# One DMA per v pair, quartered first weights, split zero fills, later loads of the second expert and a halved last tile in a sparse-attention and mixture kernel

## The chip, the cores and the metric

The kernel runs on one core of a Trainium2 chip. The metric is the device time of one execution, in microseconds (us). Before the change it was 744.33 us, the median of 3 runs (744.23 to 744.38).

The engines are called as the profile calls them: PE (TensorE matmul), PEld (its weight load), DVE (VectorE), ACT (ScalarE), POOL (GpSimd), SP (SyncE). Every run here was fast: none was over 1.5% above the fastest of its kernel. Within the fast runs there is still one difference that matters for a change of 0.3%: each run lists its mean granted TensorE clock, and some show 0.988 to 0.998 instead of 0.999 to 1.000. I call runs at 0.999 and above "full-clock" runs and always say when I use only those.

## The reference, cut to what matters

```python
# attention: 4 batches, 8 heads, 768 positions, 64 columns
k_sum = k.reshape(B, H, nb, 32, D).max(axis=3)       # block maxima of k
v_sum = v.reshape(B, H, nb, 32, D).mean(axis=3)      # block means of v
# scores: a window of |i - j| < 16, and the 24 blocks; one softmax over both
out = softmax([local scores, block scores + log(32)]) @ [v, v_sum]
# experts: x = out as 3072 x 512, E = 8, F = 1024
P = sinkhorn(exp(x @ w_gate), 8 rounds)
for e in range(8):
    out += P[:, e:e+1] * (relu(x @ w1[e]) @ w2[e])
```

## The kernel before

The heads are taken in 16 pairs. All work of the attention, of expert 0 and of the normalisation of P is put in order at build time by a small planner: each unit has an engine, an estimated cost and dependencies, and each engine then runs its own list in that fixed order. Experts 1 to 7 follow as a plain loop.

The parts that change:

```python
        def load_v(i):                                   # two DMAs per pair, one per head
            b, h0 = i // PB, (i % PB) * 2
            for j in range(2):
                nc.gpsimd.dma_start(out=v_x[i % NQ][:, :, j, 0:D],
                                    in_=v[b, h0 + j].rearrange("(g p) d -> p g d", p=128))
        # ...
        def keep_busy(n):                                # an idle (filler) matmul
            t = bank("m", "idle")
            for _ in range(n):
                nc.tensor.matmul(t[:], lhsT=zeros[:, 0:128], rhs=zeros[:], start=True, stop=True)
        nc.vector.memset(zeros, 0.0)
        keep_busy(14)                                    # 14 at the start
        # ...
        def late_constants():                            # one block on DVE
            for t in E_e:
                nc.vector.memset(t[64:128, :, :], 0.0)
            for t in V_e:
                nc.vector.memset(t[:], 0.0)
                nc.vector.memset(t[0:24, :, D:VD], 32.0)
                nc.vector.memset(t[32:56, :, VD + D:2 * VD], 32.0)
            nc.vector.memset(col_en, float(E) / float(N))
        # ...
        load(("w1", 0), lambda: load_w1(0, 0, 2), 0.85, 2.5)     # expert 0's w1 in halves
        for i in range(PB):
            load_pair(i, "r")                                    # second half of q
        load(("w1", 1), lambda: load_w1(0, 1, 2), 0.85, 2.5)
        # ...
        def transposed():                # POOL touches pair 12's k and q, then loads expert 1
            r = (NP - 4) % NB
            nc.gpsimd.tensor_copy(out=warm[:, 0:1], in_=kT[r][0:1, 0:1])
            nc.gpsimd.tensor_copy(out=warm[:, 1:2], in_=qT[r][0:1, W:W + 1])
        # ...
        plan.idle = (0.43, lambda: keep_busy(2), U["rl", 0, 0])  # planner: two fillers where
                                                                 # it foresees a gap over 0.43
        # ...
            yp = mps.tile([128, 512], FP32, tag="m", name="yps")     # experts 1 to 7, one tile
            project_mm(e, yp, h, c, range(KF))
            nc.vector.scalar_tensor_tensor(out=out_acc[:, t, :], in0=yp[:],
                                           scalar=P_sb[:, t, e:e + 1], in1=out_acc[:, t, :],
                                           op0=ALU.mult, op1=ALU.add)
            if e == E - 1:
                nc.sync.dma_start(out=out[t * 128:(t + 1) * 128, :], in_=out_acc[:, t, :])
```

The softmax here doesn't subtract the row's maximum and nothing guards it: scores larger than these inputs give would overflow.

Of the kernel before, what the change touches and what calls it, by code (L numbers as in the profile page):

```python
# [9 lines left out]
FP32 = mybir.dt.float32  # L10
BF16 = mybir.dt.bfloat16
AF = mybir.ActivationFunctionType
ALU = mybir.AluOpType
# [99 lines left out]
def kernel(  # L113
# [10 lines left out]
    nc = tc.nc  # L124

    B, H, S, D = q.shape
    G = S // 128
# [31 lines left out]
    col_en = const.tile([128, 128], FP32)  # L159
    warm = const.tile([1, 8], FP32)  # L160
    zeros = const.tile([128, 512], BF16)
# [46 lines left out]

    def project_mm(e, yp, h, c, fs):
        for f in fs:  # L210
            nc.tensor.matmul(yp[:], lhsT=h[:, f, c * 128:(c + 1) * 128],  # L211
                             rhs=w2s[e][:, f, :], start=(f == 0), stop=(f == KF - 1))

# [6 lines left out]
    with tc.tile_pool(name="attn", bufs=1) as attn, \  # L220
# [7 lines left out]
        ksT = [attn.tile([128, 128], BF16, name=f"ksT{i}") for i in range(NB)]  # L228
        v_x = [attn.tile([128, G, 2, VD], BF16, name=f"vx{i}") for i in range(NQ)]

# [36 lines left out]
        def load_v(i):  # L267
            b, h0 = i // PB, (i % PB) * 2
            for j in range(2):
                nc.gpsimd.dma_start(out=v_x[i % NQ][:, :, j, 0:D],  # L270
                                    in_=v[b, h0 + j].rearrange("(g p) d -> p g d", p=128))

# [55 lines left out]
        def block_sums(i):  # L328
            sv = v_x[i % NQ]
            vs = at["vs", i] = bank("a", "vs")[:, 0:2 * D]  # L330
            for g in range(G):
                nc.tensor.matmul(vs.rearrange("p (j d) -> p j d", j=2), lhsT=m_blk[:, g, :],  # L332
                                 rhs=sv[:, g, :, 0:D], start=(g == 0), stop=(g == G - 1))

# [11 lines left out]
        def near_values(i):  # L346

            sv, ve = v_x[i % NQ], V_e[i % NE]
            eng = nc.sync if i < BY_DMA else nc.gpsimd
            for j in range(2):  # L350
                c0, q0 = VD * j, 64 + 32 * j
                eng.dma_start(out=ve[q0 + W:q0 + 2 * W, 1:G, c0:c0 + VD],
                              in_=sv[128 - W:128, 0:G - 1, j, :])
                eng.dma_start(out=ve[q0:q0 + W, 0:G - 1, c0:c0 + VD],
                              in_=sv[0:W, 1:G, j, :])

# [47 lines left out]
        def values(i, h):  # L404
            sv, ee, ve, em = v_x[i % NQ], E_e[i % NE], V_e[i % NE], at["em", i]
            av = at["av", i, h] = bank("a", "av")
            for cc in range(HG):
                c, o = HG * h + cc, cc * 2 * VD
                for j in range(2):
                    nc.tensor.matmul(av[:, o + j * VD:o + (j + 1) * VD],  # L410
                                     lhsT=em[:, j, c, :], rhs=sv[:, c, j, :],
                                     start=(cc == 0 and j == 0), stop=False,
                                     skip_group_check=True)
            for cc in range(HG):
                c, o = HG * h + cc, cc * 2 * VD
                nc.tensor.matmul(av[:, o:o + 2 * VD], lhsT=ee[:, c, :], rhs=ve[:, c, :],  # L416
                                 start=False, stop=True, skip_group_check=True)
# [46 lines left out]
        def values_h(i, h):  # L464
            sv, em, es = v_x[i % NQ], E_h[(PB * h + i) % NEH], at.pop(("es", i, h))
            av = at["av", i, h] = bank("a", "av")

            def mm(p0, p1, cc, j, lhsT, rhs, n=VD, start=False, stop=False):
                o = cc * 2 * VD + j * VD
                nc.tensor.matmul(av[p0:p1, o:o + n], lhsT=lhsT, rhs=rhs, start=start, stop=stop,  # L470
                                 skip_group_check=True)

            for cc in range(HG):
                for j in range(2):
                    mm(0, 128, cc, j, em[:, j, cc, 2 * W:2 * W + 128], sv[:, HG * h + cc, j, :],
                       start=(cc == 0 and j == 0))
            for cc in range(HG):
                c = HG * h + cc
                for j in range(2):
                    if c + 1 < G:  # L480
                        mm(96, 128, cc, j, em[0:32, j, cc + 1, 0:32], sv[0:32, c + 1, j, :])
                    if c > 0:
                        mm(0, 32, cc, j, em[96:128, j, cc - 1 if cc else HG, LIVE:PADL],
                           sv[96:128, c - 1, j, :])
            for cc in range(HG):
                mm(0, 128, cc, 0, es[:, cc, :], V_s[i][:], n=2 * VD, stop=True)
# [129 lines left out]

        def late_constants():
            for t in E_e:
                nc.vector.memset(t[64:128, :, :], 0.0)
            for t in V_e:  # L620
                nc.vector.memset(t[:], 0.0)
                nc.vector.memset(t[0:24, :, D:VD], 32.0)
                nc.vector.memset(t[32:56, :, VD + D:2 * VD], 32.0)
            nc.vector.memset(col_en, float(E) / float(N))

# [9 lines left out]
        def load_pair(i, parts="kqv"):  # L635
            old = i - NQ
            for c in parts:
                if c == "v":
                    load(("v", i), lambda: load_v(i), 1.65, 1.75,
                         [U.get(("A", old, 1)), U.get(("near", old))])  # L640
                elif i < PB and c in "qr":
                    h = "qr".index(c)
                    load(("q", i, h), lambda h=h: load_qk(i, 1, h), 0.65, 0.6)
                else:
                    z = "kq".index(c)
                    load((c, i), lambda z=z: load_qk(i, z), 0.75 if i < PB else 1.65,
                         1.1 if i < PB else 1.55, [U.get(("tr", old, z)), U.get(("tr", old, 2))])

        def pair_start(i, prio):
# [9 lines left out]
            for z in range(0 if i >= BY_DMA else 1 if i < PB else 2):  # L659
# [9 lines left out]
            U["vs", i] = add("PE", 0.4, lambda: block_sums(i),  # L669
                             [U["v", i]] + ([U.get(("A", i - NE, 1))] if i >= PB else []), prio + 0.01, opens=[buf])  # L670
            U["Vs", i] = add("DVE", 0.22 if i < PB else 0.7, lambda: block_out(i), [U["vs", i]],
# [35 lines left out]
        def pair_whole(i, prio):  # L707
            U["near", i] = add("SP" if i < BY_DMA else "POOL", 2.4 if i < BY_DMA else 3.0, lambda: near_values(i),
                               [U["v", i], U.get(("A", i - NE, 1))], prio, lag=3.5)
            x1 = []  # L710
# [14 lines left out]
            for h in range(2):  # L725
                U["mk", i, h] = add("DVE", 0.56, lambda h=h: masks(i, h),
                                    [U["X", i, h], *x1[:h], U.get(("A", i - 2, 1))], prio)
            U["ed", i] = add("DVE", 0.78, lambda: edges(i),
                             [U["X", i, 0], U["X", i, 1], U["mk", i, 1], U.get(("A", i - NE, 1))], prio)
            for h in range(2):  # L730
# [22 lines left out]
        def expert0(t0, xs):  # L753
            key, n = t0, len(halves)
            halves.append(key)
            pr = 1000.0 + n
            w = [U["w1", 0], U["w1", 1]]
            evac, old = [], [U.get(("pj", halves[n - 2], c)) for c in range(HG)] if n >= 2 else []
            for f in range(KF):
                buf = Buffer("m")  # L760

                def fn(f=f):
                    at["hp", key, f] = hidden0(key, t0, f)
                m = add("PE", 0.67, fn, xs + [w[f // 4]] + old, pr + f * 0.01, opens=[buf])

# [30 lines left out]
        load_pair(3, "v")  # L796
        load(("w1", 0), lambda: load_w1(0, 0, 2), 0.85, 2.5)
        for i in range(PB):
            load_pair(i, "r")
        load(("w1", 1), lambda: load_w1(0, 1, 2), 0.85, 2.5)  # L800
        load("w2", lambda: load_w2(0), 0.85, 5.0)
        add("DVE", 4.0, constants, [], -5.0)
        for i in range(PB):
            pair_start(i, i)
            pair_half(i, 0, i)
        add("DVE", 1.8, late_constants, [U["A", PB - 1, 0]], 5.5)
        expert0(0, [U["x", i, 0] for i in range(PB)])
# [14 lines left out]
        def transposed():  # L822

            r = (NP - 4) % NB
            nc.gpsimd.tensor_copy(out=warm[:, 0:1], in_=kT[r][0:1, 0:1])
            nc.gpsimd.tensor_copy(out=warm[:, 1:2], in_=qT[r][0:1, W:W + 1])

        last[0] = add("POOL", 0.3, transposed, [last[0]] + [U["kT", NP - 4, z] for z in range(2)])
        load("w1n", lambda: load_w1(1), 0.85, 5.0)
# [28 lines left out]
    def step2(e, n):  # L858
        h = hs.pop((e, n))
        for c in range(4):  # L860
            t = 4 * n + c
            if e == 1:
                nc.vector.tensor_scalar_mul(out=out_acc[:, t, :], in0=out_acc[:, t, :],
                                            scalar1=P_sb[:, t, 0:1])
            yp = mps.tile([128, 512], FP32, tag="m", name="yps")
            project_mm(e, yp, h, c, range(KF))
            nc.vector.scalar_tensor_tensor(out=out_acc[:, t, :], in0=yp[:],  # L867
                                           scalar=P_sb[:, t, e:e + 1], in1=out_acc[:, t, :],
                                           op0=ALU.mult, op1=ALU.add)
            if e == E - 1:  # L870
                nc.sync.dma_start(out=out[t * 128:(t + 1) * 128, :], in_=out_acc[:, t, :])

# [35 lines left out]
```

## Time and profile before

| | before |
|---|---|
| time, median | 744.33 us |
| span of the profiled run | 742.2 us |
| first hidden matmul of expert 0 | 25.4 us |
| first hidden matmul of expert 1 | 157.7 us |
| end of the last matmul to end of span | 4.15 us |

From the profile page of before (line 1 is the span; then PE's busy time; then its busy tenths and the granted clock in 40 slices):

```profile
span 742.2 us, 10242 instructions
...
PE 729.8 (98%) x4292; PEld 358.3 (48%) x4364; DVE 373.5 (50%) x734; ACT 201.0 (27%) x343; POOL 90.6 (12%) x118
...
PE   8999999999999999999999999999999999999997
...
PEclk9999999999999999999999999999999999999999
```

PE is 90% busy or more in all slices but the first and the last. The Trainium skill says that this is not the whole story ("Trainium Kernel Development and Optimization", "Best Practices": the distance to roofline is not to be judged by matmul busy time). I use the pitch, the time from one matmul's start to the next: 32 matmuls of 512 columns take 6.91 us in the chain, 0.216 us each, which agrees with the gap that "TensorE: Matmul & The Clock Gate" (Part 1, "Wait — 56ns, not 53.3ns?") gives for a warm array (N/2.4 + 2.5 ns).

Busy time by stretches of before, in us. The columns are the length, then busy time and (instructions) of PE, PEld, DVE, ACT and POOL, the granted clock, the DMA engines' mean busy time and GB/s:

```profile
core 0: us, PE busy (x) PEld busy (x) DVE busy (x) ACT busy (x) POOL busy (x), PEclk, DMA share, GB/s
0.00:31.50 31.50, 27.35 (x398) 16.06 (x401) 22.99 (x113) 17.82 (x29) 23.57 (x37) 1.00 1.35 150
31.50:92.00 60.50, 59.86 (x721) 39.91 (x724) 55.48 (x147) 43.65 (x73) 54.57 (x69) 1.00 1.89 122
92.00:155.00 63.00, 62.34 (x536) 38.15 (x541) 45.53 (x122) 37.98 (x73) 1.56 (x2) 1.00 0.22 37
155.00:700.00 545.00, 542.37 (x2477) 247.11 (x2526) 232.74 (x332) 96.76 (x163) 10.92 (x11) 1.00 0.16 28
```

The slack is in the first line: PE is idle 4.15 us of 31.5 us there. Do not read the last line as 2.6 us of idle time in experts 1 to 7. The trace of before has 4292 matmul records beside 4364 weight loads, one of which belongs to each matmul, and a missing record looks like a short gap. The same holds for 25 recorded idle matmuls of 28 issued.

POOL's issues of loads at the start of before (start, duration, engine, line, operation, tile):

```profile
2.72 1.67 POOL L270 DMA_DIRECT2D vx_109<-in_v_dram  x2
...
4.69 0.74 POOL L258 DMA_DIRECT2D kst<-in_k_dram  x1
...
8.01 1.68 POOL L270 DMA_DIRECT2D vx_110<-in_v_dram  x2
...
10.34 0.66 POOL L258 DMA_DIRECT2D qst<-in_q_dram  x1
```

Two v issues take 1.67 us together, and k and q of the following pairs stand behind them.

The chain of waits of before (start, duration, what) has the zero fills as a block on DVE from 24.16 to 26.72 us, around the first work of expert 0 (25.41 us) and just before a masked product ("av") that waits for DVE:

```profile
24.16 0.38 DVE Ee_122 L619
...
24.56 0.38 DVE Ee_123 L619
...
25.84 0.39 DVE Ve_125 L621
...
26.72 0.41 DVE qT_97 L202
...
27.75 0.93 PE av L470 x19
```

Then the first hidden matmul of expert 0 and of expert 1, from the timeline of PE of before, and the last tile's end, with the last eviction on DVE:

```profile
25.41 0.82 PE L206 MATMUL hps<-xT,w_402 128*128 128x384 bf16 x4
```

```profile
157.74 2.54 PE L206 MATMUL hps<-xT,w_2019 128*128 128x512 bf16 x11
```

```profile
733.79 4.26 PE L211 MATMUL yps<-w_5682,h 128*128 128x512 bf16 x18
...
738.10 0.75 DVE L867 SCALAR_TENSOR_TENSOR out_acc<-yps,P_sb,out_acc 128x512 f32<-128x512 f32 x1 [0.97 <-PE yps L211]
```

A store of the output takes 2.0 us from issue to landing, the median of 24 (the list of DMA issues of before; the columns are tile, queue, count, size, us to landing):

```profile
out_dram<-out_acc SPq DMA_DIRECT2D x24, 256.0 KB, 2.0
```

### The profile page before, as it was taken

What the parts mean: (1) busy time and instruction counts of PE and PEld (TensorE: products, weight loads), DVE (VectorE), ACT (ScalarE), POOL (GpSimd) and SP (SyncE); (2) the same over time, 40 slices, a digit from 0 to 9 for tenths busy, and PEclk for the clock granted to TensorE, in tenths of its full rate; (3) what the DMA queues carried; (4) which work ended last, traced back from release to release, by engine and by line L of the source; (5) the groups of instructions that cost most, each with busy time, mean ns of one, the idle gap of its engine ahead of it and who ended that gap; (6) DMA issues with size and microseconds to landing.
All of it is one profiled execution on the core that took longest, in us unless ns stands there. A gap on an engine that the chain in (4) does not pass through costs nothing.

```text
span 742.2 us, 10242 instructions
## 1 busy us (share of the span) xinstructions
PE 729.8 (98%) x4292; PEld 358.3 (48%) x4364; DVE 373.5 (50%) x734; ACT 201.0 (27%) x343; POOL 90.6 (12%) x118
## 2 busy tenths in 40 slices
PE   8999999999999999999999999999999999999997
PEld 4666666544444444444444444444444444444443
DVE  7789976783444444444444444444444444444443
ACT  5677676442112112111111111121121121121120
POOL 8599700010000000000000000000000000000000
PEclk9999999999999999999999999999999999999999
DMA  9999970060003300213003300212003300001212
GB/s 123 169 130 129 103 119 2 1 104 10 1 1 57 57 1 0 35 29 51 1 1 57 58 1 0 49 28 38 1 1 57 57 1 0 1 1 65 92 72 113
DMA packets 86669, 33.68 MB, mean 45 GB/s; under 512 B 68704, under 2 KB 79968, under 8 KB 86624
## 3 DMA queue, kind: packets, MB, share of 16 engines
q0 software_dynamic: 78032, 26.22, 32.7%
q1 hardware_dynamic: 8064, 6.80, 3.0%
q8 instruction: 34, 0.56, 0.3%
q14 instruction: 11, 0.09, 0.0%
q10 hardware_dynamic: 528, 0.02, 0.0%
HBM read 52.45 MB, written 6.29 MB: 79 GB/s over the span
## 4 chain that ended last, share of the span: by engine, by line
PE 93%; DVE 6%; issue 1%
PE hps L206 44%; PE yps L211 43%; DVE xs L501 1%; PE idle L570 1%; PE tkq L283 1%; DVE ks_103 L315 1%; PE av L470 1%; PE sg L324 1%; PE tx L508 1%; PE ss L422 1%; DVE em L387 1%; PE vs L332 1%; PE av L410 0%; PE av L416 0%; DVE xT L202 0%
## 5 line engine op out<-in xcount | busy, mean ns | idle before, releaser
L197 ACT ACTIVATE h<-hps 128x512 bf16<-128x512 f32 (+1 forms) x220 | 125.8, 572 | 478.9 <-PE hps L206 461.9
L211 PEld LDWEIGHTS <-h 128*128 128x128 bf16 x1536 | 149.8, 98 | 175.7
L867 DVE SCALAR_TENSOR_TENSOR out_acc<-yps,P_sb,out_acc 128x512 f32<-128x512 f32 x168 | 126.2, 751 | 166.4 <-PE yps L211 158.5
L199 DVE TENSOR_SCALAR h<-hps 128x512 bf16<-128x512 f32 (+1 forms) x180 | 122.8, 682 | 169.7 <-PE hps L206 169.4
L206 PE MATMUL hps<-xT,w_402 128*128 128x384 bf16 x256 | 48.2, 326 | 0.0
L211 PE MATMUL yps<-w_514,h 128*128 128x512 bf16 x177 | 44.5, 379 | 0.7
L206 PE MATMUL hps<-xT,w_5680 128*128 128x512 bf16 x189 | 42.3, 379 | 0.2
L211 PE MATMUL yps<-w_2042,h 128*128 128x512 bf16 x189 | 42.3, 379 | 0.2
L206 PE MATMUL hps<-xT,w_3528 128*128 128x512 bf16 x189 | 42.3, 379 | 0.2
L211 PE MATMUL yps<-w_4606,h 128*128 128x512 bf16 x188 | 42.2, 379 | 0.3
L211 PE MATMUL yps<-w_4068,h 128*128 128x512 bf16 x189 | 42.3, 379 | 0.2
L206 PE MATMUL hps<-xT,w_4066 128*128 128x512 bf16 x188 | 42.2, 379 | 0.2
L206 PE MATMUL hps<-xT,w_2966 128*128 128x512 bf16 x188 | 42.2, 379 | 0.2
L211 PE MATMUL yps<-w_5144,h 128*128 128x512 bf16 x188 | 42.2, 379 | 0.2
L211 PE MATMUL yps<-w_2968,h 128*128 128x512 bf16 x187 | 42.2, 379 | 0.3
L206 PE MATMUL hps<-xT,w_5142 128*128 128x512 bf16 x189 | 42.3, 379 | 0.2
L206 PE MATMUL hps<-xT,w_4604 128*128 128x512 bf16 x187 | 42.0, 379 | 0.2
L211 PE MATMUL yps<-w_3530,h 128*128 128x512 bf16 x188 | 42.0, 379 | 0.2
L211 PE MATMUL yps<-w_5682,h 128*128 128x512 bf16 x187 | 41.8, 379 | 0.2
L206 PE MATMUL hps<-xT,w_2019 128*128 128x512 bf16 x188 | 41.9, 379 | 0.2
L206 PEld LDWEIGHTS <-w_402 128*128 128x128 bf16 x256 | 23.7, 99 | 13.1
L206 PEld LDWEIGHTS <-w_2966 128*128 128x128 bf16 x192 | 18.8, 98 | 22.6
(249 smaller groups left out, 582.8 us busy)
## 6 DMA issues: line engine op xcount, KB each, us to landing
out_dram<-out_acc SPq DMA_DIRECT2D x24, 256.0 KB, 2.0
qst<-in_q_dram POOLq DMA_DIRECT2D x32, 96.0 KB, 4.3
kst<-in_k_dram POOLq DMA_DIRECT2D x24, 96.0 KB, 4.6
w_402<-in_moe_w_dram POOLq DMA_DIRECT2D x2, 512.0 KB, 8.2
w_514<-in_moe_w_dram POOLq DMA_DIRECT2D x1, 1024.0 KB, 12.4
w_2019<-in_moe_w_dram POOLq DMA_DIRECT2D x1, 1024.0 KB, 8.2
w_2042<-in_moe_w_dram POOLq DMA_DIRECT2D x1, 1024.0 KB, 12.5
w_2966<-in_moe_w_dram POOLq DMA_DIRECT2D x1, 1024.0 KB, 8.0
```

The lines of the kernel that those rows point to most:

```text
L197: nc.scalar.activation(out=out, in_=in_, func=AF.Relu, bias=0.0, scale=1.0)
L199: nc.vector.tensor_scalar_max(out=out, in0=in_, scalar1=0.0)
L206: nc.tensor.matmul(hp[:, 0:n], lhsT=w1s[e][:, dk, f * 128:(f + 1) * 128], rhs=xT[:, dk, t0:t0 + n], start=(dk == 0), stop=(dk == KD - 1))
L211: nc.tensor.matmul(yp[:], lhsT=h[:, f, c * 128:(c + 1) * 128], rhs=w2s[e][:, f, :], start=(f == 0), stop=(f == KF - 1))
L283: nc.tensor.transpose(t[:, g * 128:(g + 1) * 128], st[:, g, :, :].rearrange("p j d -> p (j d)"), ident)
L315: nc.vector.tensor_reduce(out=ks[i % 2][:, 0, 0:24], in_=kT[r][:].rearrange("p (n w) -> p n w", w=32), axis=AX.X, op=ALU.max)
L324: nc.tensor.matmul(dst, lhsT=kT[r][p0:p0 + 64, g * 128:(g + 1) * 128], rhs=qT[r][p0:p0 + 64, g * 128 + l0:g * 128 + l1], start=True, stop= ...
L332: nc.tensor.matmul(vs.rearrange("p (j d) -> p j d", j=2), lhsT=m_blk[:, g, :], rhs=sv[:, g, :, 0:D], start=(g == 0), stop=(g == G - 1))
L387: nc.vector.tensor_tensor(out=at["em", i][:, :, c, :], in0=at["er", i][:, :, c, W:W + 128], in1=band[:, None, None, W:W + 128].to_broadcas ...
L422: nc.tensor.matmul(ss[:, 0:HS], lhsT=ksT[r][:], rhs=qT[r][:, W + h * HS:W + (h + 1) * HS], start=True, stop=True)
L470: nc.tensor.matmul(av[p0:p1, o:o + n], lhsT=lhsT, rhs=rhs, start=start, stop=stop, skip_group_check=True)
L867: nc.vector.scalar_tensor_tensor(out=out_acc[:, t, :], in0=yp[:], scalar=P_sb[:, t, e:e + 1], in1=out_acc[:, t, :], op0=ALU.mult, op1=ALU.add)
```

## The change

Its words are: one DMA for v of a pair; transposes all on PE; expert 0's w1 in quarters; expert 1's loads wait for the last near rows; last tile in column halves. In fact, all transposes are on PE before too. The words do not mention that the zero fills are split as well. (Near rows are the rows of v beside each group of 128 positions, which are copied by DMA for the local window.) The core of the diff, with cuts:

```diff
-        v_x = [attn.tile([128, G, 2, VD], BF16, name=f"vx{i}") for i in range(NQ)]
+        v_x = [attn.tile([128, 2, G, VD], BF16, name=f"vx{i}") for i in range(NQ)]
         def load_v(i):
-            for j in range(2):
-                nc.gpsimd.dma_start(out=v_x[i % NQ][:, :, j, 0:D],
-                                    in_=v[b, h0 + j].rearrange("(g p) d -> p g d", p=128))
+            nc.gpsimd.dma_start(
+                out=v_x[i % NQ][:].rearrange("p j g x -> p (j g) x")[:, :, 0:D],
+                in_=v[b, h0:h0 + 2].rearrange("j (g p) d -> p (j g) d", p=128))
  ...  (v_x is indexed accordingly in six other places)
-        def late_constants():  ... all fills in one unit
+        def edge_constants(n):   nc.vector.memset(E_e[n][64:128, :, :], 0.0)  ... col_en for n == 0
+        def value_constants(n):  t = V_e[n]; ... the three fills of t
-                    load(("v", i), lambda: load_v(i), 1.65, 1.75,
+                    load(("v", i), lambda: load_v(i), 0.95, 1.75,          # planned cost
  ...
-        load(("w1", 0), lambda: load_w1(0, 0, 2), 0.85, 2.5)
-        for i in range(PB):
-            load_pair(i, "r")
-        load(("w1", 1), lambda: load_w1(0, 1, 2), 0.85, 2.5)
+        for n in range(4):
+            load(("w1", n), lambda n=n: load_w1(0, n, 4), 0.85, 1.25)
+            if n == 1:
+                for i in range(PB):
+                    load_pair(i, "r")
  ...
-        add("DVE", 1.8, late_constants, [U["A", PB - 1, 0]], 5.5)
+        for n in range(NE):
+            U["ec", n] = add("DVE", 0.42, lambda n=n: edge_constants(n), [U["A", PB - 1, 0]], 15 + n)
+            U["vc", n] = add("DVE", 0.5, lambda n=n: value_constants(n), [U["A", PB - 1, 0]], 15.5 + n)
  ...
-            r = (NP - 4) % NB
+            r = (NP - 1) % NB          # pair 15 instead of 12, and its near rows too
+            ve = V_e[(NP - 1) % NE]
+            for j in range(2):
+                nc.gpsimd.tensor_copy(out=warm[:, 2 + j:3 + j],
+                                      in_=ve[64 + 32 * j:96 + 32 * j, G - 2, VD * j:VD * j + 1])
  ...
-            yp = ...; project_mm(e, yp, h, c, range(KF)) ...
+            parts = 2 if (e, t) == (E - 1, NT - 1) else 1
+            for d0 in range(0, DM, DM // parts):
+                d = slice(d0, d0 + DM // parts)
+                yp = ...; project_mm(e, yp, h, c, range(KF), d)
+                ...  evict d; store d, the second half on ACT's queue
```

More of the change, by code (lines that the diff above doesn't have):

```diff
@@ L159 @@
     col_en = const.tile([128, 128], FP32)
-    warm = const.tile([1, 8], FP32)
+    warm = const.tile([32, 8], FP32)
     zeros = const.tile([128, 512], BF16)
@@ L207, in hidden_mm, with project_mm @@
                              rhs=xT[:, dk, t0:t0 + n], start=(dk == 0), stop=(dk == KD - 1))
-    def project_mm(e, yp, h, c, fs):
+    def project_mm(e, yp, h, c, fs, d=slice(0, 512)):
         for f in fs:
-            nc.tensor.matmul(yp[:], lhsT=h[:, f, c * 128:(c + 1) * 128],
-                             rhs=w2s[e][:, f, :], start=(f == 0), stop=(f == KF - 1))
+            nc.tensor.matmul(yp[:, d], lhsT=h[:, f, c * 128:(c + 1) * 128],
+                             rhs=w2s[e][:, f, d], start=(f == 0), stop=(f == KF - 1))
     NQ = 6
@@ L332, in block_sums @@
                 nc.tensor.matmul(vs.rearrange("p (j d) -> p j d", j=2), lhsT=m_blk[:, g, :],
-                                 rhs=sv[:, g, :, 0:D], start=(g == 0), stop=(g == G - 1))
+                                 rhs=sv[:, :, g, 0:D], start=(g == 0), stop=(g == G - 1))
         def block_out(i):
@@ L352, in near_values @@
                 eng.dma_start(out=ve[q0 + W:q0 + 2 * W, 1:G, c0:c0 + VD],
-                              in_=sv[128 - W:128, 0:G - 1, j, :])
+                              in_=sv[128 - W:128, j, 0:G - 1, :])
                 eng.dma_start(out=ve[q0:q0 + W, 0:G - 1, c0:c0 + VD],
-                              in_=sv[0:W, 1:G, j, :])
+                              in_=sv[0:W, j, 1:G, :])
         def scores(i):
@@ L410, in values @@
                     nc.tensor.matmul(av[:, o + j * VD:o + (j + 1) * VD],
-                                     lhsT=em[:, j, c, :], rhs=sv[:, c, j, :],
+                                     lhsT=em[:, j, c, :], rhs=sv[:, j, c, :],
                                      start=(cc == 0 and j == 0), stop=False,
@@ L474, in values_h @@
                 for j in range(2):
-                    mm(0, 128, cc, j, em[:, j, cc, 2 * W:2 * W + 128], sv[:, HG * h + cc, j, :],
+                    mm(0, 128, cc, j, em[:, j, cc, 2 * W:2 * W + 128], sv[:, j, HG * h + cc, :],
                        start=(cc == 0 and j == 0))
@@ L480, in values_h @@
                     if c + 1 < G:
-                        mm(96, 128, cc, j, em[0:32, j, cc + 1, 0:32], sv[0:32, c + 1, j, :])
+                        mm(96, 128, cc, j, em[0:32, j, cc + 1, 0:32], sv[0:32, j, c + 1, :])
                     if c > 0:
                         mm(0, 32, cc, j, em[96:128, j, cc - 1 if cc else HG, LIVE:PADL],
-                           sv[96:128, c - 1, j, :])
+                           sv[96:128, j, c - 1, :])
             for cc in range(HG):
@@ L615, in constants, with edge_constants, value_constants @@
             nc.vector.tensor_copy(out=wg_bf[:], in_=wg_f32[:])
-        def late_constants():
-            for t in E_e:
-                nc.vector.memset(t[64:128, :, :], 0.0)
-            for t in V_e:
-                nc.vector.memset(t[:], 0.0)
-                nc.vector.memset(t[0:24, :, D:VD], 32.0)
-                nc.vector.memset(t[32:56, :, VD + D:2 * VD], 32.0)
-            nc.vector.memset(col_en, float(E) / float(N))
+        def edge_constants(n):
+            nc.vector.memset(E_e[n][64:128, :, :], 0.0)
+            if n == 0:
+                nc.vector.memset(col_en, float(E) / float(N))
+        def value_constants(n):
+            t = V_e[n]
+            nc.vector.memset(t[:], 0.0)
+            nc.vector.memset(t[0:24, :, D:VD], 32.0)
+            nc.vector.memset(t[32:56, :, VD + D:2 * VD], 32.0)
         U = {}
@@ L669, in pair_start @@
             U["vs", i] = add("PE", 0.4, lambda: block_sums(i),
-                             [U["v", i]] + ([U.get(("A", i - NE, 1))] if i >= PB else []), prio + 0.01, opens=[buf])
+                             [U["v", i]] + ([U.get(("A", i - NE, 1)), U["vc", i % NE]] if i >= PB else []), prio + 0.01, opens=[buf])
             U["Vs", i] = add("DVE", 0.22 if i < PB else 0.7, lambda: block_out(i), [U["vs", i]],
@@ L708, in pair_whole @@
             U["near", i] = add("SP" if i < BY_DMA else "POOL", 2.4 if i < BY_DMA else 3.0, lambda: near_values(i),
-                               [U["v", i], U.get(("A", i - NE, 1))], prio, lag=3.5)
+                               [U["v", i], U.get(("A", i - NE, 1)), U["vc", i % NE]], prio, lag=3.5)
             x1 = []
@@ L728, in pair_whole @@
             U["ed", i] = add("DVE", 0.78, lambda: edges(i),
-                             [U["X", i, 0], U["X", i, 1], U["mk", i, 1], U.get(("A", i - NE, 1))], prio)
+                             [U["X", i, 0], U["X", i, 1], U["mk", i, 1], U.get(("A", i - NE, 1)), U["ec", i % NE]], prio)
             for h in range(2):
@@ L756, in expert0 @@
             pr = 1000.0 + n
-            w = [U["w1", 0], U["w1", 1]]
+            w = [U["w1", n] for n in range(4)]
             evac, old = [], [U.get(("pj", halves[n - 2], c)) for c in range(HG)] if n >= 2 else []
@@ L763, in fn @@
                     at["hp", key, f] = hidden0(key, t0, f)
-                m = add("PE", 0.67, fn, xs + [w[f // 4]] + old, pr + f * 0.01, opens=[buf])
+                m = add("PE", 0.67, fn, xs + [w[f // 2]] + old, pr + f * 0.01, opens=[buf])
                 def ev(f=f):
@@ L822, in transposed @@
         def transposed():
-            r = (NP - 4) % NB
-            nc.gpsimd.tensor_copy(out=warm[:, 0:1], in_=kT[r][0:1, 0:1])
-            nc.gpsimd.tensor_copy(out=warm[:, 1:2], in_=qT[r][0:1, W:W + 1])
-        last[0] = add("POOL", 0.3, transposed, [last[0]] + [U["kT", NP - 4, z] for z in range(2)])
+            r = (NP - 1) % NB
+            nc.gpsimd.tensor_copy(out=warm[:, 0:1], in_=kT[r][0:32, 0:1])
+            nc.gpsimd.tensor_copy(out=warm[:, 1:2], in_=qT[r][0:32, W:W + 1])
+            ve = V_e[(NP - 1) % NE]
+            for j in range(2):
+                nc.gpsimd.tensor_copy(out=warm[:, 2 + j:3 + j],
+                                      in_=ve[64 + 32 * j:96 + 32 * j, G - 2, VD * j:VD * j + 1])
+        last[0] = add("POOL", 0.3, transposed, [last[0], U["near", NP - 1]] + [U["kT", NP - 1, z] for z in range(2)])
         load("w1n", lambda: load_w1(1), 0.85, 5.0)
@@ L864, in step2 @@
                                             scalar1=P_sb[:, t, 0:1])
-            yp = mps.tile([128, 512], FP32, tag="m", name="yps")
-            project_mm(e, yp, h, c, range(KF))
-            nc.vector.scalar_tensor_tensor(out=out_acc[:, t, :], in0=yp[:],
-                                           scalar=P_sb[:, t, e:e + 1], in1=out_acc[:, t, :],
-                                           op0=ALU.mult, op1=ALU.add)
-            if e == E - 1:
-                nc.sync.dma_start(out=out[t * 128:(t + 1) * 128, :], in_=out_acc[:, t, :])
+            parts = 2 if (e, t) == (E - 1, NT - 1) else 1
+            for d0 in range(0, DM, DM // parts):
+                d = slice(d0, d0 + DM // parts)
+                yp = mps.tile([128, 512], FP32, tag="m", name="yps")
+                project_mm(e, yp, h, c, range(KF), d)
+                nc.vector.scalar_tensor_tensor(out=out_acc[:, t, d], in0=yp[:, d],
+                                               scalar=P_sb[:, t, e:e + 1], in1=out_acc[:, t, d],
+                                               op0=ALU.mult, op1=ALU.add)
+                if e == E - 1:
+                    (nc.scalar if d0 else nc.sync).dma_start(out=out[t * 128:(t + 1) * 128, d],
+                                                             in_=out_acc[:, t, d])
     for si, (e, n) in enumerate(steps):
```

## The prediction

> **What bounds the kernel.** TensorE: the page shows PE busy 729.8 of 742.2 us at full clock. The Trainium skill ("Trainium Kernel Development and Optimization", "Best Practices") warns that matmul busy time is a bad metric, so I count columns: in the chain of waits 32 matmuls of 512 columns take 6.91 us, 0.216 us each, which is what "TensorE: Matmul & The Clock Gate" gives for a warm array (512/2.4 + 2.5 ns). Experts 1 to 7 are 2688 such matmuls, 580 us; they start at about 155 us and only the last tile changes. So the change works in the first 155 us and the last 6.
>
> Slack there, from busy time by stretches: from 0 to 31.5 us PE is busy 27.35 us (1.3 us of the gap is start-up); from 31.5 to 155 us it is idle only 1.3 us. Also 28 idle (keep-warm) matmuls run, 14 of them after the start; these cost about 3 us at 0.216. So at most about 7 us can be won.
>
> **What changes.** Despite its words, transposes do not move: all pairs are on PE already.
> 1. v in one DMA: Pool issues two per pair in 1.65 us; I estimate 1.0 for one (other issues take 0.6 to 0.9). Pool issues back to back from 34 to 86 us, but PE is filled by expert 0 then (waits list: 0.3 us for a v load), so only the first pairs matter: their k and q come 0.7 to 2 us earlier.
> 2. The zero fills of edge and value tiles, a block on DVE at 24.2 to 26.7 us on the chain, are split and interleaved. DVE work is the same; the 0.8 us weight-load wait for the mask at 27.7 should shrink.
> 3. The scheduler puts in 22 idle matmuls instead of 28: 6 x 0.216 = 1.3 us, if PE does not just wait instead.
> 4. w1 in quarters: the first half already lands at 22.4 us, before its use at 25.4; freedom, not time.
> 5. Expert 1's loads wait for pair 15's near rows (issued 107.8 to 110.4): they start at about 113 instead of 91 us and take 8 and 12.5 us, so they land by about 127, before their use at 155. No stall. Near rows of pair 13 no longer share DMA with them (5.5 us landing against 2.5 for others); PE hardly waited: at most 0.3 us.
> 6. Last tile in halves: 16 matmuls of 256 columns cost the same 1.7 us; the last eviction (0.75 us, DVE) becomes about 0.4, the last store is half as large: about 0.2 less of 2.0. About 0.5 us.
>
> **Sum on the critical path:** idle matmuls -1.3, gaps at 7 to 28 us -0.5, later gaps -0.2, tail -0.5: -2.5 us.
>
> **Prediction: 741.8 us**, 8 in 10 between 740.2 and 743.8. Faster by over 2%: 0.01; within 2%: 0.98; slower by over 2%: 0.01.
>
> **What would show it.** Right: expert 1's first hidden matmul about 2 us earlier; 22 idle matmuls and no more PE idle time before 31.5 us than now; expert loads issued near 111 us with no PE wait for them; one v issue of about 1.0 us; last eviction near 0.4 us and last PE matmul to the end of span about 3.5 instead of 4.1 us. Wrong: PE waits for v of pair 0 or 1 (block sums now come before summaries); v issue still 1.6 us; PE idle at 31 to 155 us grown, as DVE is 92% busy from 31.5 to 92 us.
>
> **What could make it wrong.** The head may be bound by DVE/ACT latency, so that removing idle matmuls only uncovers gaps: then about 743.5. Or the new order in the first half shortens more than counted: near 740. A missed weight load at 155 us would cost several us; I see none.

## The result, and the profile after

The changed kernel took 742.12 us, the median of 4 runs (741.55 to 743.85), against 744.30 for the 4 runs of before. The ratio is 0.9975 with a 95% interval of 0.9957 to 0.9992. Ratios are the mean time of one kernel's fast runs over that of the other's of the same rounds, so not quite the ratio of the medians. It is inside the 2% band, and the time is inside the predicted range (741.8; 740.2 to 743.8).

| | before | after |
|---|---|---|
| median | 744.30 | 742.12 |
| span of the profiled run | 742.2 | 739.8 |
| expert 0 begins | 25.4 | 22.3 |
| expert 1 begins | 157.7 | 155.9 |
| expert 1's begin to the end of the span | 584.5 | 583.9 |
| idle matmuls issued | 28 | 22 |

The page of the changed kernel, its first two lines (the clock row is all nines, as before):

```profile
span 739.8 us, 10282 instructions
...
PE 732.2 (99%) x4366; PEld 358.6 (48%) x4366; DVE 373.1 (50%) x735; ACT 201.3 (27%) x343; POOL 82.8 (11%) x106
```

The higher busy share here is partly an artefact: this trace has every matmul record (4366), the other does not. The span is what counts.

The same stretches of the changed kernel:

```profile
0.00:31.50 31.50, 28.69 (x419) 17.18 (x420) 24.99 (x118) 19.04 (x31) 23.75 (x37) 1.00 1.45 156
31.50:92.00 60.50, 59.62 (x719) 39.78 (x717) 54.42 (x146) 44.21 (x73) 44.55 (x52) 1.00 1.87 119
92.00:155.00 63.00, 62.69 (x532) 37.55 (x531) 45.76 (x122) 37.21 (x72) 3.58 (x7) 1.00 0.25 41
155.00:700.00 545.00, 545.00 (x2526) 247.06 (x2525) 231.64 (x330) 96.11 (x161) 10.93 (x11) 1.00 0.16 28
```

The first stretch has gained: PE is busy 28.69 us instead of 27.35, with fewer fillers in it (three fillers of before have no record, so a part of the difference is an artefact). The middle has not. Both kernels stand at about 1.2 to 1.3 us of idle time from 31.5 to 155 us, where before's figure is raised by missing records.

POOL's issues at the start of the changed kernel:

```profile
2.72 1.04 POOL L269 DMA_DIRECT2D vx_109<-in_v_dram  x1
...
4.12 0.71 POOL L258 DMA_DIRECT2D kst<-in_k_dram  x1
...
7.43 1.05 POOL L269 DMA_DIRECT2D vx_110<-in_v_dram  x1
...
9.14 0.64 POOL L258 DMA_DIRECT2D qst<-in_q_dram  x1
```

One v DMA takes 1.04 us instead of 1.67 for two, so k of pair 1 goes out 0.57 us earlier, v of pair 1 0.58 us and q of pair 3 1.2 us (the prediction had 0.7 to 2). Not everything lands earlier: the first pair's v, now one load of twice the size, lands 5.9 us after its issue, at 8.6 us, while the two halves of before had landed by 8.3 us. Pair 1's v lands at 13.6 us, and at 14.0 us or later in before. The first hidden matmuls of expert 0 and expert 1:

```profile
22.31 0.82 PE L206 MATMUL hps<-xT,w_347 128*128 128x384 bf16 x4
```

```profile
155.90 4.48 PE L206 MATMUL hps<-xT,w_2427 128*128 128x512 bf16 x20
```

Expert 0 begins 3.1 us earlier, expert 1 only 1.84 us earlier. The difference is no loss by itself, since the order around these points differs; only at expert 1's begin have both kernels done the same useful work.

The chain of waits of the changed kernel now runs through POOL's issues and the landing of pair 1's v:

```profile
6.85 0.59 POOL qst L258
7.43 6.14 DMA vx_110<-in_v_dram
...
13.62 0.50 PE vs L332 x6
```

Block sums ("vs") of pair 1 start at 13.62 us, when that DMA, issued at 7.43 us, has landed. Up to there the chain is POOL and v. The wait of PE for a mask behind the zero-fill block (0.4 us at 27.75 us in before) is no longer listed, but the chain still passes through two of the four split units on DVE, from 21.27 to 22.56 us.

The end of the changed kernel, and its DMA issues for v and for the last tile:

```profile
736.27 0.48 DVE L879 SCALAR_TENSOR_TENSOR out_acc<-yps,P_sb,out_acc 128x256 f32<-128x256 f32 x1 [0.39 <-PE yps L211]
736.79 0.36 ACTq L883 DMA_DIRECT2D out_dram<-out_acc  x1
```

```profile
vx_109<-in_v_dram POOLq DMA_DIRECT2D x3, 192.0 KB, 5.9
...
out_dram<-out_acc SPq DMA_DIRECT2D x1, 128.0 KB, 1.8
out_dram<-out_acc ACTq DMA_DIRECT2D x1, 128.0 KB, 1.8
```

The last eviction is 0.48 us instead of 0.75, the last store lands in 1.8 us instead of 2.0, and the span ends about 3.55 us after the last matmul's end instead of 4.15.

Expert 1's loads are now issued at 116 us, from POOL's timeline of the changed kernel:

```profile
115.97 0.76 POOL L187 DMA_DIRECT2D w_2427<-in_moe_w_dram  x1
116.72 0.90 POOL L193 DMA_DIRECT2D w_2449<-in_moe_w_dram  x1
```

They take 8.0 and 13.6 us to land, and the first use is at 155.9 us, so PE does not wait for them.

### The profile page after: what moved, and what is told of

The parts are those of the page before. It is cut to its first block, busy times and chain, and to the rows that moved or that the text cites. A ratio compares the mean times of both kernels' runs of the same rounds, so it can differ in the third digit from the quotient of the medians.

```text
span 739.8 us, 10282 instructions
## 1 busy us (share of the span) xinstructions
PE 732.2 (99%) x4366; PEld 358.6 (48%) x4366; DVE 373.1 (50%) x735; ACT 201.3 (27%) x343; POOL 82.8 (11%) x106
## 4 chain that ended last, share of the span: by engine, by line
PE 93%; DVE 4%; DMA 1%; POOL 1%; issue 0%; POOLq 0%
PE hps L206 44%; PE yps L211 44%; DMA vx_110<-in_v_dram 1%; DVE xs L501 1%; PE tkq L283 1%; PE sg L324 1%; PE ss L422 1%; PE av L470 1%; PE tx L508 1%; PE vs L332 1%; DVE em L387 1%; DVE ks_103 L315 0%; DVE ks_104 L315 0%; PE av L416 0%; PE av L410 0%
## 5 line engine op out<-in xcount | busy, mean ns | idle before, releaser
L879 DVE SCALAR_TENSOR_TENSOR out_acc<-yps,P_sb,out_acc 128x512 f32<-128x512 f32 (+1 forms) x169 | 126.4, 748 | 165.9 <-PE yps L211 165.8
L211 PE MATMUL yps<-w_501,h 128*128 128x512 bf16 x192 | 46.2, 379 | 0.0
L211 PE MATMUL yps<-w_2947,h 128*128 128x512 bf16 x192 | 42.4, 379 | 0.0
L211 PE MATMUL yps<-w_4047,h 128*128 128x512 bf16 x192 | 42.4, 379 | 0.0
L211 PE MATMUL yps<-w_2449,h 128*128 128x512 bf16 x192 | 42.4, 379 | 0.0
L211 PE MATMUL yps<-w_4585,h 128*128 128x512 bf16 x192 | 42.4, 379 | 0.0
L211 PE MATMUL yps<-w_5123,h 128*128 128x512 bf16 x192 | 42.4, 379 | 0.0
L211 PE MATMUL yps<-w_3509,h 128*128 128x512 bf16 x192 | 42.4, 379 | 0.0
L211 PE MATMUL yps<-w_5661,h 128*128 128x512 bf16 (+1 forms) x200 | 42.3, 370 | 0.0
## 6 DMA issues: line engine op xcount, KB each, us to landing
w_2449<-in_moe_w_dram POOLq DMA_DIRECT2D x1, 1024.0 KB, 13.6
```

Of the source, the lines that this page charges most:

```text
L211: nc.tensor.matmul(yp[:, d], lhsT=h[:, f, c * 128:(c + 1) * 128], rhs=w2s[e][:, f, d], start=(f == 0), stop=(f == KF - 1))
L879: nc.vector.scalar_tensor_tensor(out=out_acc[:, t, d], in0=yp[:, d], scalar=P_sb[:, t, e:e + 1], in1=out_acc[:, t, d], op0=ALU.mult, op1=A ...
```

## The experiments

All kernels gave correct results. Each was timed in 5 rounds. The three batches (e1 to e4, e5 to e8, e9 to e12) ran on three different chips, each with runs of before beside them. The runs of before in the three batches had medians of 744.15, 744.17 and 744.20 us. Of these 33 runs, 25 were at full clock, with a mean of 744.08 us, and 8 below it (0.996 to 0.998), at 745.2 to 746.4 us. So a run of before at a lowered clock takes 1.1 to 2.3 us more, and that is one run in four, and the mean differences below are read beside the full-clock ones.

| run | what | median (us) | ratio to before, 95% interval | full-clock runs: mean (number) |
|---|---|---|---|---|
| before | | 744.17 | | 744.08 (25 of 33) |
| changed | | 741.95 | 0.9962 [0.995, 0.9975], again alone | 742.00 (8 of 9) |
| e1 | before + halves | 743.45 | 0.9994 [0.9981, 1.0008] | 743.46 (5 of 6) |
| e2 | before + one v DMA | 742.02 | 0.9972 [0.996, 0.9983] | 742.19 (6 of 6) |
| e3 | before + split fills | 744.45 | 1.0007 [0.9994, 1.002] | 744.25 (4 of 6) |
| e4 | changed, two v DMAs, order kept | 745.46 | 1.0013 [0.9998, 1.0027] | 743.35 (1 of 6) |
| e6 and e12 | before + one v DMA + halves | 741.28 | 0.9966 [0.9946, 0.9987] and 0.9964 [0.9948, 0.9979] | 741.29 (8 of 11) |
| e7 | changed without the 8 later fillers | 741.84 | 0.996 [0.9946, 0.9974] | 741.50 (3 of 5) |
| e8 | changed, v planned to land later | 742.27 | 0.9975 [0.996, 0.9989] | 742.22 (5 of 6) |
| e9 | before without the 14 later fillers | 746.56 | 1.0029 [1.0016, 1.0043] | none of 5 |
| e10 | changed with the fills in one block | 741.31 | 0.9969 [0.9951, 0.9987] | 741.17 (4 of 6) |
| e11 | changed, expert 1 loaded early | 741.59 | 0.9961 [0.9949, 0.9973] | 741.73 (5 of 5) |

The theory after the result was this: POOL's shorter issue of v brings the loads of the first pairs earlier, and this shortens real waits of PE; the column halves give the tail. The rivals were that the split fills, the changed order, or the smaller number of idle matmuls bring the gain.

### e1: the column halves alone

```diff
 (before, with the last hunk of the change)
+            parts = 2 if (e, t) == (E - 1, NT - 1) else 1
```

> The kernel before with the last tile's column halves alone. My sum (tail worth 0.5 us): 743.8, and in the profile the time from the last matmul's end to the end of the span 3.5 instead of 4.1 us, with the head unchanged (expert 1 begins within 0.2 us of before). Rival, that the split changes nothing because the last store's fixed cost rules: 744.3.

Measured: 743.45 us, at full clock 0.6 us below before. In the profiled run expert 1 begins at 157.83 us, as before, and the last matmul starts at 737.90 us (737.69 in before) in a span of 741.8 (742.2). The tail is worth its 0.6 us on its own, a little more than the 0.5 predicted. The interval of all runs includes 1, because one of the six runs had a lower clock, so it rests on the full-clock runs (743.29 to 743.70, all below before's median).

### e2: the single v DMA alone

```diff
 (before, with load_v, the v_x layout, and the planned cost 0.95 of the change)
```

> The kernel before with the single v DMA (and its planned cost) alone; the planner then puts in 22 idle matmuls, as in the changed kernel. If the single DMA is what shortens the head, nearly all of the head's 1.8 us comes here: 742.5 to 742.8. Rival, that the split of the zero fills brings it: 744.0 or more here, with gaps in place of the six idle matmuls.

Measured: 742.02 us, the whole gain of the head, and below the expected range (at full clock 1.88 us under before's 744.07 of the same chip). This program too has 22 idle matmuls by its plan. Its profiled run was the slowest of its six, 743.45 us at full clock, and shows long waits for v. From the waits of PE between 5 and 31.5 us (total us, times, longest):

```profile
PE vs L332 <- DMA vx<-in_v_dram: 2.4, 4, 1.0
```

Block sums waited four times for v, 2.4 us in all, 1.0 us at the longest. The changed kernel's run shows 0.7 us of such waits, and its repeat's profile none. So the spread of the new kernels at full clock (741.55 to 743.85) may come from the landing of v. That is argued and not shown: no fast run of e2 and not the slow run of the changed kernel has a trace, and e11's profiled run waited 1.3 us for v and still took 741.91 us.

### e3: the split zero fills alone

```diff
-        add("DVE", 1.8, late_constants, [U["A", PB - 1, 0]], 5.5)
+        (the four units of the change)
```

> The kernel before with the split zero fills alone; still 28 idle matmuls. My theory: a small part, 743.8 to 744.2, since DVE work is the same. Rival, that the 2.5 us block on DVE was what held the head: 742.5.

Measured: 744.45 us, and 744.25 at full clock against 744.08. No gain, and just above the expected range of 743.8 to 744.2. The block of 2.5 us on DVE stood on the chain of before, but in e3's profile PE waits for other things in the same stretch instead: 1.1 us for v, 1.0 us for an exponential on ACT and 0.6 us for q, none of which it waited for that long in before. Expert 0 began at 26.7 us, not earlier than before's 25.4. A place on the chain was no cost that could be saved by itself.

### e4: two v DMAs in the changed kernel's order

```diff
 (the changed kernel)
-            nc.gpsimd.dma_start(  ... both heads
+            for j in range(2):
+                nc.gpsimd.dma_start(  ... head j          # planned cost left at 0.95
 (and v_x in before's layout)
```

> The changed kernel, its order on every engine kept (22 idle matmuls), but v loaded by two DMAs again. It tells Pool's time from the order. If earlier loads are the cause, PE now waits for v and for k and q in the first 22 us and loses 1 to 2 us: 743.2 to 744.2, with expert 1 starting near 157. If only the order and the fewer idle matmuls matter, it stays at 742.1.

Measured: 745.46 us, above the expected range, 3.5 us above the changed kernel and 1.3 above before. The order of PE, with its 22 idle matmuls, is the changed kernel's. The halved last tile, worth 0.6 us by e1, is still in, so order and fewer fillers alone bring nothing; POOL's time is needed. The layout of v_x goes back too, but it is no rival: with either layout (before, and the changed kernel) a matmul that reads v takes 0.22 us for block sums and 0.19 us for the products. The timeline of PE shows the waits, with what ended them in brackets:

```profile
13.94 0.52 PE L332 MATMUL vs<-vx,m_blk 128*128 128x128 bf16 x6 [0.79 <-DMA vx<-in_v_dram]
...
15.96 0.85 PE L280 MATMUL tkq<-ident,kst 128*64 128x128 bf16 x12 [1.18 <-DMA kst<-in_k_dram]
```

The last of these, transposes of pair 3's k, starts at 14.37 us in the changed kernel's trace, so PE is 1.6 us late at 15.96 us. Nearly all of that time the clock was full. This is the cost of two issues in this order, read from two traces of the same sequence.

Then something happened that was not expected. The stretches around it:

```profile
12.60:16.00 3.40, 1.44 (x26) 0.90 (x22) 3.05 (x9) 2.04 (x3) 3.25 (x5) 0.98 1.87 158
16.00:22.80 6.80, 6.44 (x70) 4.32 (x72) 3.63 (x10) 2.81 (x5) 4.14 (x7) 0.51 1.76 161
22.80:26.00 3.20, 3.02 (x66) 2.10 (x66) 2.15 (x6) 1.07 (x3) 2.56 (x4) 1.00 1.31 169
```

In the 3.4 us before 16.0 us PE was busy 1.44 us, and at about 15.8 us the clock was halved for 6.8 us. Five of the six runs had a clock of 0.994 to 0.998 and took 744.7 to 746.4 us; the one at 0.999 took 743.35. That single run puts the waits at 1.4 us (743.35 against 742.00), which agrees with the 1.6 us of the traces and with the prediction's own fear of 743.5 if gaps are only uncovered. The five others took 1.4 to 3 us more than it.

### e5: the changed kernel again

> The changed kernel again, as the yardstick of these four on one chip. Expected 742.1 as on record, with runs up to about 743.9 at full clock (waits for a late v).

Measured: 741.76 us (741.31 to 742.17). The gain repeats, 2.4 us between the medians of one chip's runs, and none of these five runs was near the 743.9 that was expected as possible.

### e6 and e12: the single v DMA and the halves, twice

```diff
 (before, with the v hunks and the last-tile hunk, nothing else)
```

> The kernel before with the single v DMA and the column halves only. If the two parts add up (2.1 and 0.7 us measured alone) and quarters, split fills and the later load of expert 1 bring nothing: 741.4, at or below the changed kernel. Rival, that the other three parts bring a share: over 742.1.

> The single v DMA and the halves only, once more on the chip of these runs: 741.2 at full clock, if it really is the fastest; 741.8 or more if the 0.6 us to the changed kernel was chance.

Measured: 741.17 us and 741.67 us. At full clock the two runs' mean is 741.29 (8 of 11 runs), 0.7 us below the changed kernel's. But 3 of 11 runs had a lower clock (741.8, 743.9 and 745.9 us), against 1 of 9 of the changed kernel (742.3). Over all runs the means are 741.99 and 742.03 us. So the two parts hold the whole gain, and I do not claim that this version beats the changed kernel.

### e7 and e9: without the fillers

```diff
-        plan.idle = (0.43, lambda: keep_busy(2), U["rl", 0, 0])
+        plan.idle = None        # e7 in the changed kernel, e9 in before; the first 14 stay
```

> The changed kernel without the 8 idle matmuls after the start. If each idle matmul costs its 0.216 us on the path (as my prediction counted them), it gains up to 1.7 us: 740.4. If they only stand in gaps that the data leave anyway, the time stays within 0.3 us of the changed kernel's. If they hold the clock, the clock falls below 0.999 in some runs and those take 1 to 3 us more.

> The kernel before without the 14 idle matmuls after the start. In the changed kernel, taking out 8 brought nothing (741.84 against 741.76). If they stand in gaps here too: within 0.3 us of before at full clock (744.1), perhaps with more runs at a lowered clock and then 1 to 3 us slower. If my step, 0.216 us each on the path, were right: 741.2.

Measured: 741.84 us in the changed kernel, which is no gain against 741.76 for 8 fillers less (1.7 us at 0.216 each). In before, 746.56 us: taking 14 fillers out cost 2.4 us. All five runs had a lowered clock (0.988 to 0.995), so no run gives the time at full clock. The profiled run does, up to the fall: PE runs before's sequence without the fillers, and the products ("av") of pair 3 start at 22.46 us, against 22.27 us in before. Without the fillers PE is no earlier, and 0.2 us late. The next "av" starts at 29.87 us against 27.75, so the loss came while the clock was halved. The stretches of that run:

```profile
13.20:16.60 3.40, 2.35 (x53) 1.59 (x49) 3.15 (x7) 1.94 (x3) 3.07 (x5) 1.00 2.23 149
16.60:20.00 3.40, 2.36 (x45) 1.53 (x43) 3.05 (x9) 2.71 (x6) 2.34 (x5) 1.00 1.67 177
20.00:23.50 3.50, 2.65 (x50) 1.98 (x50) 2.04 (x6) 1.08 (x2) 1.63 (x3) 0.93 1.24 175
...
22.90:23.20 0.30, 0.30 (x12) 0.24 (x7) 0.12 (x1) 0.00 (x0) 0.00 (x0) 0.67 1.29 204
...
23.50:30.30 6.80, 6.55 (x81) 3.72 (x81) 4.06 (x15) 4.48 (x8) 4.63 (x6) 0.53 1.22 185
30.30:34.00 3.70, 3.70 (x65) 2.55 (x60) 2.84 (x7) 2.25 (x4) 0.44 (x1) 1.00 2.27 158
```

The clock halved at about 23.0 us (it is 0.67 from 22.90 to 23.20). From 19.6 to 23.0 us PE was busy 2.15 us. With the fillers in, before's runs mostly keep the clock (25 of 33). So an idle matmul is not a cost on the path. It stands in a gap that the data leave anyway, and in before it pays by holding the clock. In the changed kernel the later fillers are not missed: two of e7's five runs had a clock of 0.998 and took 741.84 and 741.85 us, 0.3 more than the mean of the other three.

In the profiled run of e12 one long wait precedes the fall. Its stretches before and in the drop:

```profile
7.40:10.80 3.40, 2.02 (x51) 1.49 (x47) 2.12 (x6) 2.13 (x3) 3.40 (x6) 0.99 1.40 171
11.30:21.60 10.30, 9.94 (x123) 7.02 (x123) 7.69 (x20) 5.81 (x8) 6.37 (x10) 0.53 1.63 183
```

After 2.02 busy us of 3.4, with a wait of 1.4 us for v of one pair, the clock was halved from about 10.7 to 21.0 us. That run took 743.88 us.

No threshold follows from this. The busy time in some 3.4 us before the three falls is 1.6 (e4), 2.0 (e12) and 2.15 us (e9), but other stretches of 3.4 us kept the full clock with as little: 1.76 us in e3 (from 11.6 us), 1.92 in e2 (from 16.6 us) and 1.96 in e9 itself (from 6.4 us). What decides between them stays open.

### e8: v planned to land later

```diff
-        U[key] = add("LAND", 0, None, [last[1]], lag=1.0)
+        U[key] = add("LAND", 0, None, [last[1]], lag=2.0 if key[0] == "v" else 1.0)
```

> The changed kernel with the planner told that v lands 1 us later, so block sums move behind the scores (24 idle matmuls). If the waits of PE for v in the first 22 us cost time and make the spread: 741.2 to 741.8 and a spread under 1 us at full clock. Rival, that v's waits only replace other waits: no change, 742.1.

Measured: 742.27 us, no better than the changed kernel. PE's waits for v were 0.3 us in the profile (0.7 in the changed kernel's), and waits for DVE stood in the same stretch: 0.8 us for block maxima, 0.7 for normalised rows, 0.6 for masks. The full-clock spread was 741.92 to 742.60; that is hardly tighter than the repeat e5 on the same chip (741.31 to 742.17). The rival was right about the time: other waits stand where the waits for v were.

### e10: the fills in one block again

```diff
 (the changed kernel, with late_constants of before as one unit)
```

> The changed kernel with the zero fills as one block again (so single v DMA, halves, quarters and the later load of expert 1). If the split fills are what makes the changed kernel 0.6 us slower than v and halves alone: 741.2. If quarters or the later load cost it: 741.8.

Measured: 741.31 us, and 741.17 at full clock, 0.8 below the changed kernel and level with v and halves alone. So quarters and the later load cost nothing. Against e11 of the same batch (split fills, 741.73 at full clock) the split fills seem to cost about half a microsecond at full clock; that is not firm, since e11 also loads expert 1 earlier, and over all runs e11 has the lower mean (741.73 against 742.12). Two of the six runs had a clock of 0.995 and took 743.8 and 744.3 us. Whether the split fills make a lowered clock rarer can't be settled with these numbers: at 0.998 or below stand 5 of 23 runs with the single v DMA and whole fills (e2, e6, e10, e12), against 1 of 14 with split fills, fillers and the planned landing left as they are (the changed kernel and e11).

### e11: expert 1 loaded early again

```diff
 (the changed kernel)
-            r = (NP - 1) % NB   ... and the near rows of pair 15
+            r = (NP - 4) % NB
```

> The changed kernel with expert 1's loads not waiting for pair 15's near rows. My prediction: at most 0.3 us either way, 741.5 to 742.1; in the profile the loads start near 85 us instead of 116 us. Rival, that sharing the DMA engines with near rows stalls PE: 742.5 or more.

Measured: 741.59 us, 0.2 below the changed kernel's repeat at 741.76, with loads issued at 87.0 us instead of 116. The wait is worth nothing either way.

## Why the prediction was right, and which term was not

- **The time.** 741.8 predicted, 742.12 measured. The two sums agree too: head -2.0 predicted, -1.84 measured at expert 1's begin; tail -0.5 predicted, -0.6 measured.
- **"Idle matmuls -1.3".** This term named the wrong thing. Six fillers fewer do not save six times 0.216 us: e7 took out eight more and gained nothing, and e9 took fourteen out of before and lost 2.4 us. What the runs showed in its place is that the loads of the first pairs come earlier (e2: 2.1 us from the single v DMA alone; e4: with two DMAs in the same order it is lost), so the gaps are shorter, and the planner, which foresees this, puts fewer fillers in. At full clock, before's PE is no earlier without its fillers (22.46 us against 22.27 at the same instruction). That the number came out right all the same fits a planner that foresees the gaps about right; that is argued, not shown, so the match of the sum is in part luck.
- **"Gaps at 7 to 28 us -0.5", with the zero-fill block as a main part.** The split fills gave nothing (e3: 744.25 against 744.08 at full clock). The gain in this stretch came with the earlier loads.
- **v in one DMA, 1.0 us estimated.** 1.04 us measured. That only the first pairs matter agrees with the stretches: POOL has 10 us less work from 31.5 to 92 us (54.57 to 44.55), and PE is no less idle there. The Trainium skill ("DMA: Bandwidth & Descriptors", "Anatomy of one DMA") says that many descriptors can be emitted before their cost shows; here twice the rows in one DMA took 1.04 us where one half takes 0.85, so most of an issue did not grow with its rows.
- **Quarters bring no time; expert 1's later loads stall nothing.** Both hold (e10, e11). The loads began at 116 us, not at the predicted 113, and the margin to 155.9 us is wide.
- **The tail.** The last eviction took 0.48 us instead of the predicted 0.4, the store was 0.2 us shorter as predicted, and it came to 0.6 us in all (e1).
- **The stated risk.** "PE waits for v of pair 0 or 1" did come true, with 0.3 and 0.4 us in the profiled run, and did not eat the gain. The other stated risk, that taking out idle matmuls only uncovers gaps (743.5), is what e4 shows when the loads come late. The risk that I did not state was the clock.

Left open: whether the single DMA gains in before's order too (it was not run, so the DMA and the order that the planner makes of it are shown only together), whether the split fills protect the clock, and how much idle time lowers it.

## What to carry to other kernels

Count a filler matmul as the sign of a gap and not as its cost: take it out in a run before crediting its removal. Look at the engine that issues the loads when it works back to back at the start: here one issue in place of two gave the head's whole gain, while relieving DVE gave none. The same saving later, under a full PE, left PE's idle time as it was. When the effect looked for is below 0.5%, sort runs by granted clock before comparing them, and give all runs beside that: in e4 and e9 the lowered clock was a part of what the edit did.

## What the Trainium skill lacked or had wrong

- "TensorE: Matmul & The Clock Gate", Part 1, has the clock fall back to half "after ≥1 idle window (~3.4µs)". It tells elsewhere in Part 1 of falls through frequent short idle times, but not how much busy time still holds the clock. Here it fell after 1.6 busy us of some 3.4 (e4), 2.0 (e12) and 2.15 (e9), and held after 1.76 (e3), 1.92 (e2) and 1.96 (e9). These are the profile's busy times.
- The same table has it return "After ≥1 busy SHORT window (~3.4µs sustained)". Here a fall lasted 6.8 us (e4, e9) and 10.2 us (e12), in e12 with PE recorded as busy throughout the first 6.8 us. The runs with a lowered clock took mostly 1 to 3 us more than the full-clock runs of the same kernel, and 4.6 at most (e6).
- "DMA: Bandwidth & Descriptors" gives no issue time on POOL by the number of rows: here 1.04 us for a v load of 12 x 128 rows, and 1.67 us for two of 6 x 128.
- Its fit in "Anatomy of one DMA" (2.0 us plus the bytes over 436e3) is for one DMA. It would give about 2.5 us for a v load of 192 KB, an estimate from that page; here the median from issue to landing was 5.9 to 8.2 us, by buffer, in a queue with others ahead. No run here shows such a load alone, so the fit is not tested; the page lacks what a filled queue adds.
